# Softmax sums of a unit's pairs in one block of matmuls, V's product by row halves, output tiles copied by two engines

## The chip, the cores and the metric

The kernel runs on one core of a Trainium2 chip. The metric is the device time of one execution in microseconds (us), as the median of several runs.

## What is computed

Attention with normalised queries and keys over 8 batches of 12 heads, 448 positions and 64 columns a head, and behind it a two-layer block with the activation h cos h:

```python
q_n = q / (norm(q) + 1e-06); k_n = k / (norm(k) + 1e-06)     # 8 x 12 x 448 x 64
attn = softmax(q_n @ k_n^T / tau)                            # tau = 0.1
x = (attn @ v) as rows of 768                                # 3584 x 768
h = x @ w_in                                                 # 768 x 2048
out = (h * cos(h)) @ w_out                                   # 2048 x 768, float32
```

## The kernel before

**Tiling.** A pair (index g, 48 of them) is two heads of one batch; three pairs make a unit (index u, 16), two units a batch (8). A sequence of 448 positions is cut into 7 blocks of 64. Six of them lie as three full chunks of 128 partitions in the tile PX (two blocks in a chunk), the seventh is spread over the two partition halves, each half holding it for half of the queries (chunk 0 in the code, view PHv, 224 columns a head).

**A pair.** `scores(g, c)` multiplies keys and queries on TensorE as four 64\*64 tiles, c = 0 for the short chunk and 1 to 3 for the full ones, into two PSUM buffers SC in turn. ScalarE takes the exponential from SC to PX (line 707). `attend(g, direct, stages)` then forms V's product and the softmax sums in the two-bank PSUM buffer AV (AVa and AVs): stages 0 and 1 are the short chunk (`rest`, line 730: V and a block of ones, 64\*64), stage 2 is V's product over the full chunks in 128\*32 column tiles (`av`, line 737) and the sums of the full chunks with ones as weights (`sm` and `sm2`, lines 745 and 753, also 128\*32). One copy of both banks, 896 wide, goes to the tile xu: on VectorE (line 817), or for the even pairs above 18 on ScalarE (line 814).

**The chain.** For the pairs not in `PLAN["direct"]`, `chain(u)` collects a unit's sums: four gather DMAs on SyncE's queue from xu to sums (line 855), an addition of two parts and a reciprocal on VectorE (lines 867 and 870; in unit 2 on GpSimd), a write to DRAM (scr, line 871), two broadcast reads into RB (line 873), and for each pair GpSimd's multiply xT = xu x RB (line 877). The direct pairs take logarithm and exponential on ScalarE instead. Some of them, in `PLAN["quarters"]`, form V's product and the sums as 64\*64 tiles by row halves (`quarter`, line 763); the pairs in `PLAN["folded"]`, at the start, form half-wide sums (`sm32`, line 771).

**The two layers.** M1 (`m1`, matmuls in line 887) multiplies a batch's xT with w_in; ScalarE's Sin (line 916) and VectorE's product (line 918) give gT. Two of M1's column groups start early, with the first three chunks of xT; their other chunks follow as xT comes. M2 multiplies gT with w_out, 32 groups of matmuls to a tile of 128 rows, in 64\*64 tiles by row halves (`m2_quarters`, line 985) or as whole tiles (line 1014). `m2_drain` copies a finished tile in two halves of 384 columns to osb on VectorE (line 952; the last of all on ScalarE, line 950), and SyncE's queue stores it. osb has three buffers.

**Order.** `pair(g, f)` writes out the order on TensorE: scores of pair g, parts of `attend(g - 1)`, and between them the shares f[0] to f[3] of M2's groups (for a middle pair 3, 2, 5 and 6). All instructions are first collected with modelled costs; `play` then plays them through and fixes each engine's order by due times. On TensorE it keeps the written order, except in the first part of the kernel (`free`), where it looks 24 operations ahead.

Of the kernel before, what the change touches and what calls it, by code (L numbers as in the profile page):

```python
# [7 lines left out]
ALU = mybir.AluOpType  # L8
# [7 lines left out]
    "ahead": (1, 2),  # L16
    "folded": (0, 1, 2, 3),
# [45 lines left out]
class Program:  # L63
# [9 lines left out]
    WINDOW = 24  # L73
    PATIENCE = 0.1
# [81 lines left out]
    def play(self):  # L156
# [63 lines left out]
        while todo:  # L220
            best = None
            for e in self.ENGINES:
                if e == "PE":
                    s = None
                    for o in pe[: self.WINDOW if pe and pe[0].free else 1]:
                        if o.free != pe[0].free:
                            break
                        if left[o.idx] == 0:
                            t = max(free[e], ready_at[o.idx])
                            if s is None or t < s - self.PATIENCE:  # L230
                                s, c = t, (t, 0, o)
# [25 lines left out]
            if e == "PE":  # L257
                pe.remove(o)
                if o.free:
                    self.gaps.append((max(free[e], 3.0), s))  # L260
                if mode is not None and mode != o.mode:
# [129 lines left out]
def bass_cosine_attention__then__act_gcu_kernel(  # L391
# [22 lines left out]
    SPR = UH * S // 128  # L414
# [4 lines left out]
    NT = 3  # L419
    TD, LT = PLAN["turned"], 9  # L420
# [27 lines left out]
    lnn = sbs("lnn", 2, [128, UH * NB], F32)  # L448
# [7 lines left out]
    sums = sbs("sums", 2, [128, 2 * SPR], F32)  # L456
    rcp = sbs("rcp", 2, [128, SPR], F32)
# [14 lines left out]
    scr = nc.dram_tensor("scr", (NU, UH * S), F32)  # L472
# [10 lines left out]
    xuv = xu.ap().rearrange("p (r g s) -> p r g s", r=5, g=UP)  # L483
# [16 lines left out]
    ISSUE = {"load": (0.62, 128), "gather": (0.64, 64), "spread": (0.4, 128), "bcast": (0.62, 64),  # L500
# [48 lines left out]
    pool(lambda e: e.memset(ones.ap().rearrange("p (x y) -> p x y", y=32)[:, 0:4:3], 0.0), (), ["zeros"], 0.12)  # L549
    sel = [gT.bitcast(F32).ap()[:, (f * RING + S) // 2 : (f * RING + S) // 2 + 128] for f in (NF - 2, NF - 1)]  # L550
# [65 lines left out]
    lnnv = [t.ap().rearrange("p (h s) -> p h s", h=UH) for t in lnn]  # L616
    rnv = [t.ap().rearrange("p (h s) -> p h s", h=UH) for t in rn]

    def rnorm(u, p0, p1, t=(0, 1)):
# [5 lines left out]
        if u in PLAN["roots"]:  # L625
# [6 lines left out]
        act(lambda e: e.activation(lnnv[i][:, h, w], n2v[i][:, h, w], ACT.Ln, bias=cst.ap()[:, 1:2]),  # L632
            [("n2", i, p, z) for p, z in keys] + ["cst1"], [("lnn", i, p, z) for p, z in keys],
            n, "E", 1, "ln" + tag)
        act(lambda e: e.activation(rnv[i][:, h, w], lnnv[i][:, h, w], ACT.Exp, scale=-0.5),  # L635
            [("lnn", i, p, z) for p, z in keys], [("rn", i, p, z) for p, z in keys], n, "E", 0, "rn" + tag)
# [47 lines left out]
    def scores(g, c):  # L684
        j, y, z = g % 2, g % NT, (c + 1) % 2
# [25 lines left out]

    def attend(g, direct, stages=(0, 1, 2)):
        u, p, j = g // UP, g % UP, g % 2
        i, y, b = u % 2, u % 3, g // PB
        AVq = AVv[:, :, 0:S].rearrange("p x (s o m) -> p x s o m", s=NB, o=2)
        ws = slice(32, 96) if direct else slice(64, 128)
# [17 lines left out]
        def av(e, c):  # L734
# [4 lines left out]
            return t  # L739

        def sm(e):
            for n in range(2):
                for a in range(2):
                    o = 64 * a + 32 * n
                    t = e.matmul(AVv[o : o + 32, 1, 0:S], ones.ap()[:, 32:64], PXv[j][:, n, a, :],
                                 start=False, stop=False)
            return t

        def sm2(e):
            for n in range(2):  # L750
                for a in range(2):
                    o, w = 64 * a + 32 * n, slice(S // 2 * n, S // 2 * n + S // 2)
                    t = e.matmul(AVv[o : o + 32, 1, w], ones.ap()[:, 32:64], PXv[j][:, 2, a, w],  # L753
                                 start=False, stop=True)
            return t
# [52 lines left out]
        if not direct:  # L808
            P.op("PE", sm, ["ones", ("PX", j, 1), ("PX", j, 2)], ["AVs"], cost=MM, mode="C32", label="S%d" % g)
            P.op("PE", sm2, ["ones", ("PX", j, 3)], ["AVs"], cost=HALF, mode="C32", label="S%d" % g)  # L810
            keep = [("xa", u % 3, p), ("xs", i, p)]
            both = bass.AP(xu, (u % 3 * UP + p) * S, [[5 * UP * S, 128], [(3 + i - u % 3) * UP * S, 2], [1, S]])
            if g % 2 == 0 and g > 3 * PB:
                act(lambda e: e.activation(both, AVv[:, :, 0:S], ACT.Copy, bias=0.0), ["AVa", "AVs"], keep, 2 * S,
                    label="xu%d" % g)
            else:
                dve(lambda e: e.tensor_copy(both, AVv[:, :, 0:S]), ["AVa", "AVs"], keep, 2 * S, label="xu%d" % g)  # L817
            return
# [3 lines left out]
        if folded:  # L822
            s, r = xuv[:, 3 + i, p, 0 : S // 2], RBv[i][:, p, 0 : S // 2]
            act(lambda e: e.activation(s, AVv[:, 1, 0 : S // 2], ACT.Ln), ["AVs"], [("xs", i, p)], S // 2, "E",
                label="lnS%d" % g, bias=PLAN["bs"])
            act(lambda e: e.activation(r, s, ACT.Exp, scale=-1.0), [("xs", i, p)], [("RB", i, p)], S // 2, "E",
# [11 lines left out]
        act(lambda e: e.activation(xuv[:, 3 + i, p, :], AVv[:, 1, 0:S], ACT.Ln), ["AVs"], [("xs", i, p)], S, "E",  # L838
            label="lnS%d" % g, bias=PLAN["bs"] if g < PB else 0.0)
        act(lambda e: e.activation(r, xuv[:, 3 + i, p, :], ACT.Exp, scale=-1.0), [("xs", i, p)], [("RB", i, p)], S, "E",  # L840
# [10 lines left out]
    def chain(u):  # L851
        i, b = u % 2, u // 2
        n = sum(UP * u + p not in PLAN["direct"] for p in range(UP))
        w = SPR // UP * n
        dma("SP", [lambda e, r=r, a=a: e.dma_start(
            sums[i].ap()[64 * a : 64 * a + 64, w * r : w * r + w],
            bass.AP(xu, ((64 * a + 32 * r) * 5 + 3 + i) * UP * S, [[5 * UP * S, 1], [w, 64], [1, w]]))
            for r in range(2) for a in range(2)], [("xs", i, p) for p in range(n)], [("sums", i)], "sums%d" % i, 0.7,
            "gather%d" % u, pad=0.0 if u in PLAN["power"] else PLAN["late"])
        r = rcp[i].ap()[:, 0:w]  # L860
        parts = sums[i].ap()[:, 0 : 2 * w].rearrange("p (r x) -> p r x", r=2)
        if u in PLAN["power"]:
            pool(lambda e: e.tensor_tensor(r, parts[:, 0], parts[:, 1], ALU.add), [("sums", i)], [("rcp", i)], 0.23, label="sum")
            pool(lambda e: e.tensor_tensor(r, r, bass.AP(cst, 2, [[4, 128], [0, w]]), ALU.pow), [("rcp", i), "cst2"], [("rcp", i)],
                 0.05 + 0.166 * w, label="recip")
        else:
            dve(lambda e: e.tensor_reduce(out=r, in_=sums[i].ap()[:, 0 : 2 * w].rearrange("p (r x) -> p x r", r=2),
                                          axis=mybir.AxisListType.X, op=ALU.add), [("sums", i)], [("rcp", i)], 2 * w,
# [205 lines left out]
    def direct(g):  # L1074
        return g in PLAN["direct"]
# [179 lines left out]
```

## Time and profile before

| | |
|---|---|
| median of 3 runs | 425.53 us (424.62 to 425.71) |
| profiled execution | span 424.5 us, first to last instruction; no other time is given for it |
| TensorE (PE) | busy 414.0 us, 98% of the span, 6077 matmuls |
| ScalarE (ACT) | 274.1 us, 65% |
| GpSimd (POOL) | 236.9 us, 56% |
| VectorE (DVE) | 189.0 us, 45% |
| DMA | 63.61 MB, 150 GB/s on average |

The span is what lies between the first and the last instruction. Engines work side by side, so their busy times do not add up. A matmul's length holds the time in which it flows through the array while the next one has started; the cost of a series is read from the starts.

### The profile page before, as it was taken

What the parts mean: (1) busy time and instruction counts of PE and PEld (TensorE: products, weight loads), DVE (VectorE), ACT (ScalarE), POOL (GpSimd) and SP (SyncE); (2) the same over time, 40 slices, a digit from 0 to 9 for tenths busy, and PEclk for the clock granted to TensorE, in tenths of its full rate; (3) what the DMA queues carried; (4) which work ended last, traced back from release to release, by engine and by line L of the source; (5) the groups of instructions that cost most, each with busy time, mean ns of one, the idle gap of its engine ahead of it and who ended that gap; (6) DMA issues with size and microseconds to landing.
All of it is one profiled execution on the core that took longest, in us unless ns stands there. A gap on an engine that the chain in (4) does not pass through costs nothing.

```text
span 424.5 us, 13591 instructions
## 1 busy us (share of the span) xinstructions
PE 414.0 (98%) x6077; PEld 234.8 (55%) x6077; DVE 189.0 (45%) x250; ACT 274.1 (65%) x363; POOL 236.9 (56%) x189
## 2 busy tenths in 40 slices
PE   8899989999999999999999999999999999999997
PEld 3454556655556555655566455655566545555565
DVE  4564744555653086225733078122852144223521
ACT  5896578884897557876588556775488735713500
POOL 4999996897833794927493395806856042020000
PEclk9999999999999999999999999999999999999999
DMA  8999999999576999589655996569955930141023
GB/s 188 250 253 224 207 215 161 195 206 231 102 107 144 201 223 186 116 193 209 155 116 86 207 229 106 133 100 224 224 111 89 147 105 2 42 120 38 2 60 90
DMA packets 81034, 63.61 MB, mean 150 GB/s; under 512 B 45776, under 2 KB 75984, under 8 KB 80976
## 3 DMA queue, kind: packets, MB, share of 16 engines
q1 hardware_dynamic: 62768, 50.06, 56.8%
q0 software_dynamic: 18048, 12.59, 19.7%
q8 instruction: 48, 0.79, 0.8%
q10 hardware_dynamic: 160, 0.10, 0.1%
q14 instruction: 10, 0.08, 0.1%
HBM read 54.98 MB, written 11.13 MB: 156 GB/s over the span
## 4 chain that ended last, share of the span: by engine, by line
PE 73%; POOL 8%; DMA 6%; issue 4%; ACT 4%; SPq 3%; DVE 2%; ACTq 0%; POOLq 0%; DVEq 0%
PE MP L985 18%; PE SC L887 17%; PE AV L887 11%; PE SC L692 5%; PE AV L737 5%; POOL qks L643 4%; PE MP L1014 4%; POOL xT L877 3%; PE SC L1014 3%; DMA RB<-scr 3%; PE MP L887 2%; PE AV L730 2%; PE AV L763 1%; DMA qkT<-qks 1%; ACT PX L707 1%
## 5 line engine op out<-in xcount | busy, mean ns | idle before, releaser
L707 ACT ACTIVATE PX<-SC 128x448 bf16<-128x448 f32 (+1 forms) x192 | 153.2, 823 | 25.8 <-PE SC L692 15.6
L985 PE MATMUL MP<-W,gT 64*64 64x384 bf16 x2816 | 142.0, 323 | 0.8 <-DVE qkT L681 0.6
L985 PEld LDWEIGHTS MP<-W,gT 64*64 64x64 bf16 x2816 | 78.7, 107 | 34.5 <-issue 3.5
L643 POOL TENSOR_TENSOR qks<-raw,rn 128x896 bf16<-128x896 f32 (+1 forms) x48 | 79.6, 1680 | 31.8 <-ACT rn L635 31.6
L887 PE MATMUL SC<-xT,W 128*128 128x448 bf16 x444 | 90.2, 352 | 0.0
L877 POOL TENSOR_TENSOR xT<-xu,RB 128x448 bf16<-128x448 f32 x34 | 37.7, 1136 | 74.7 <-DMA RB<-scr 74.7
L604 POOL TENSOR_TENSOR sq<-raw 128x896 bf16<-128x896 f32 x44 | 73.8, 1694 | 8.3 <-DMA raw<-in_q_dram 7.7
L916 ACT ACTIVATE cosb<-SC,cst 128x896 f32<-128x896 f32 x37 | 37.2, 1006 | 49.0 <-PE SC L887 44.5
L887 PEld LDWEIGHTS SC<-xT,W 128*128 128x128 bf16 x444 | 43.4, 98 | 40.2
L887 PE MATMUL AV<-xT,W 128*128 128x448 bf16 x276 | 59.7, 353 | 1.7 <-POOL xT L877 1.7
L952 DVE COPY osb<-MP 128x384 f32<-128x384 f32 x50 | 25.9, 552 | 67.0 <-PE MP L985 56.4
L611 DVE TENSOR_REDUCE n<-sq 128x14 f32<-128x896 bf16 (+2 forms) x49 | 51.4, 1055 | 6.3 <-ACT sq L602 5.2
L692 PE MATMUL SC<-qkT 64*64 64x448 bf16 x576 | 52.1, 357 | 0.4 <-ACT PX L707 0.2
L918 DVE TENSOR_TENSOR gT<-SC,cosb 128x896 bf16<-128x896 f32 x37 | 40.3, 1088 | 23.2 <-ACT cosb L916 23.1
L916 ACT ACTIVATE cosb<-AV,cst 128x896 f32<-128x896 f32 x23 | 23.1, 1006 | 35.0 <-PE AV L887 32.0
L887 PEld LDWEIGHTS AV<-xT,W 128*128 128x128 bf16 x276 | 26.0, 98 | 29.1 <-POOL xT L877 5.1
L918 DVE TENSOR_TENSOR gT<-AV,cosb 128x896 bf16<-128x896 f32 x23 | 25.0, 1088 | 27.5 <-ACT cosb L916 27.4
L817 DVE COPY xu<-AV 128x896 f32<-128x896 f32 x20 | 21.7, 1083 | 30.4 <-PE AV L753 30.3
L737 PE MATMUL AV<-PX,va 128*32 128x448 bf16 x492 | 31.0, 356 | 0.0
L692 PEld LDWEIGHTS SC<-qkT 64*64 64x64 bf16 x576 | 16.5, 105 | 17.8 <-ACT PX L707 9.9
L730 PE MATMUL AV<-PX,va 64*64 64x224 bf16 x192 | 25.7, 262 | 0.2
L730 PE MATMUL AV<-PX,ones 64*64 64x224 bf16 x192 | 25.7, 262 | 0.0
(78 smaller groups left out, 361.7 us busy)
## 6 DMA issues: line engine op xcount, KB each, us to landing
raw<-in_k_dram SPq DMA_DIRECT2D x48, 224.0 KB, 6.4
raw<-in_q_dram SPq DMA_DIRECT2D x48, 224.0 KB, 7.1
out_dram<-osb SPq DMA_DIRECT2D x54, 192.0 KB, 3.4
va<-in_v_dram POOLq DMA_DIRECT2D x32, 192.0 KB, 8.9
RB<-scr SPq DMA_DIRECT2D x18, 336.0 KB, 4.8
W<-in_moe_w_in_dram POOLq DMA_DIRECT2D x4, 768.0 KB, 14.5
W<-in_moe_w_out_dram POOLq DMA_DIRECT2D x4, 768.0 KB, 19.1
RB<-scr SPq DMA_DIRECT2D x6, 224.0 KB, 4.3
```

Source lines behind the costliest of these rows:

```text
L604: pool(lambda e, x=x, y=y: e.tensor_tensor(y, x, x, ALU.mult), src_, dst, 0.1 + n * 1.78e-3, label="sq%d.%d" % (u, p)).pad = LATE if u > 1 ...
L611: dve(lambda e, w=w: e.tensor_reduce(out=n2v[i][:, 2 * p : 2 * p + 2, w], in_=sqv[p][:, :, w, :], axis=mybir.AxisListType.X, op=ALU.add), ...
L643: f = lambda e, s0=s0, s1=s1: e.tensor_tensor(qksv[i][:, p, s0:s1].rearrange("p s h d -> p h s d"), rawv[i][:, h, s0:s1, :], bass.AP(rn[i] ...
L692: m = e.matmul(SCv[z][BP * o : BP * o + BP, a, 0:S], t[r, c - 1 + (NT3 + 1) * o, 0:BP], t[r, :, BP : 2 * BP], start=True, stop=True)
L707: act(lambda e: e.activation(PHv[j] if c == 0 else PXv[j][:, c - 1], SCv[z][:, :, 0:n], ACT.Exp, scale=1.0 / TAU), ["SC%d" % z], [("PX", j ...
L730: m = e.matmul(to, w, PHv[j][r, a, :], start=(n == 0 and g not in PLAN["quarters"]), stop=False)
L737: t = e.matmul(AVv[o : o + 32, 0, 0:S], vav[y][:, 2 * p + a, c + 1, d : d + 32], PXv[j][:, c, a, :], start=False, stop=(c == NT3 - 1))
L877: pool(lambda e, p=p: e.tensor_tensor(xTv[b % 2][:, UP * i + p, :], xuv[:, u % 3, p, :], RBv[i][:, p, :], ALU.mult), [("RB", i, p), ("xa", ...
L887: t = e.matmul(ph[:, a, 0:S], W1v[:, order[c], 128 * n : 128 * n + 128], xTv[b % 2][:, order[c], :], start=(c == 0), stop=(c == NKC - 1))
L916: act(lambda e, ph=ph, cz=cz: e.activation(cosv[cz], ph[:, :, 0:S], ACT.Sin, bias=cst.ap()[:, 0:1], scale=1.0), names(gi) + ["cst0"], [("c ...
L918: dve(lambda e, ph=ph, cz=cz, gi=gi: e.tensor_tensor(gTv[:, 2 * gi : 2 * gi + 2, S * (b % 2) : S * (b % 2) + S], ph[:, :, 0:S], cosv[cz], ...
L985: r = e.matmul(POH[b][x : x + 64, 0:HW], gTv[k, y, col + x : col + x + 64], W2v[k, y, HW * b : HW * b + HW], start=(y == 0 and h == 0), st ...
```

## The change

For the pairs that are not direct:

- V's product over the full chunks is formed in 64\*64 tiles, each half of the partitions into its own bank of AV, and the short chunk joins each bank (`split`). VectorE copies the first bank to xu and then adds the second.
- The sums are no longer formed with each pair. When a unit's last such pair has its product, `counts(u)` forms the sums of all of them, one behind the other, in one 128 by 32 column tiling: each 32-column tile holds one head and one half of the queries, 224 columns; the weight (`mark`) has ones in a few columns, so that each pair's sums land in rows of their own. One copy of 224 columns goes to xs.
- The chain then needs one gather and no addition; RB holds the halves of the queries apart, and GpSimd's multiply reads and writes by pieces of 32.
- PX has four buffers instead of two (the exponentials stay until the unit's end). Room comes from xu (3 rows for 5), osb (2 buffers for 3), the logarithms in place, and zeros that share gT.
- For output tiles 0 to 24 ScalarE copies the second half.
- `play` may take any ready one of the next 8 TensorE operations outside the free part too, and charges a change of tiling in the choice. The written order moves: f[0] and f[1] are done together before the second score, and the third score comes before stage 2.

```diff
 PLAN = {
+    "halves": tuple(range(25)),
...
+    REACH = 8
...
-                    for o in pe[: self.WINDOW if pe and pe[0].free else 1]:
+                    for o in pe[: self.WINDOW if pe and pe[0].free else self.REACH]:
                         if o.free != pe[0].free:
                             break
                         if left[o.idx] == 0:
                             t = max(free[e], ready_at[o.idx])
+                            if not o.free and mode is not None and o.mode != mode:
+                                t += self.SWITCH[o.mode]
...
-    lnn = sbs("lnn", 2, [128, UH * NB], F32)
-    PX = sbs("PX", 2, [128, NB * S], BF16)
-    xu = sb("xu", [128, 5 * UP * S], F32)
+    PX = sbs("PX", NPX, [128, NB * S], BF16)
+    xu = sb("xu", [128, 3 * UP * S], F32)
+    xs = sbs("xs", 2, [128, S // 2], F32)
-    osb = sbs("osb", 3, [128, DM], F32)
+    osb = sbs("osb", NO, [128, DM], F32)
-    zt = sb("zt", [128, S], BF16)
+    zt = gT.ap()[:, S : 2 * S]
+    mark = sb("mark", [128, 3 * 4 * 32], BF16)
...
+    dve(lambda e: e.memset(mark.ap(), 0.0), (), ["mark0"], 192)
+    for z in range(2):
+        for n, at in enumerate(((0, 24), (0, 16, 24), (8,), (16,))):
+            for x in at:
+                dve(lambda e, ...: e.memset(markv[64 * z : 64 * z + 64, 0 : z + 2 : z + 1, n, x : x + 1], 1.0), ["mark0"], ["mark"], 8)
...
+    def split(g, stages):
...
+        def tail(e):
+            for o in range(2):
+                r = slice(BP * o, BP * o + BP)
+                for a in range(2):
+                    m = e.matmul(AVq[64 * a : 64 * a + 64, o, :, o, :], vav[y][r, 2 * p + a, 0 if o else VS - 1, :],
+                                 PHv[j][r, a, :], start=False, stop=True)
+        def part(e, c):
+            for o in range(2):
+                r = slice(BP * o, BP * o + BP)
+                for a in range(2):
+                    m = e.matmul(AVv[64 * a : 64 * a + 64, o, 0:S], vav[y][r, 2 * p + a, c + 1, :], PXv[j][r, c, a, :],
+                                 start=(c == 0), stop=False)
...
+            dve(lambda e: e.tensor_copy(to, AVv[:, 0, 0:S]), ["AVa"], [("xa", u % 3, p)], S, label="xa%d" % g)
+            dve(lambda e: e.tensor_tensor(to, to, AVv[:, 1, 0:S], ALU.add), ["AVs", ("xa", u % 3, p)], [("xa", u % 3, p)], S, label="xb%d" % g)
+    def counts(u):
+        gs = [UP * u + p for p in range(UP) if UP * u + p not in PLAN["direct"]]
+        for p, g in enumerate(gs):
+            def count(e, p=p, j=g % NPX):
+                v = p + 1 if p else len(gs) == 2
+                for c in range(-1, NT3):
+                    for o in range(4):
+                        a, h = o // 2, o % 2
+                        m = e.matmul(AVv[32 * o : 32 * o + 32, 0, 0 : S // 2], markv[:, 0 if c >= 0 else 1 + h, v, :],
+                                     halved(j, c, a, h) if c >= 0 else PHv[j][:, a, :],
+                                     start=(p == 0 and c < 0), stop=(p == len(gs) - 1 and c == NT3 - 1))
+        dve(lambda e: e.tensor_copy(xs[u % 2].ap(), AVv[:, 0, 0 : S // 2]), ["AVa"], [("xs", u % 2)], S // 2, label="xs%d" % u)
...
     def attend(g, direct, stages=(0, 1, 2)):
+        if not direct:
+            split(g, stages)
+            return
...
-        if not direct:
-            P.op("PE", sm, ["ones", ("PX", j, 1), ("PX", j, 2)], ["AVs"], cost=MM, mode="C32", label="S%d" % g)
-            P.op("PE", sm2, ["ones", ("PX", j, 3)], ["AVs"], cost=HALF, mode="C32", label="S%d" % g)
-            if g % 2 == 0 and g > 3 * PB:
-                act(lambda e: e.activation(both, AVv[:, :, 0:S], ACT.Copy, bias=0.0), ["AVa", "AVs"], keep, 2 * S,
-            else:
-                dve(lambda e: e.tensor_copy(both, AVv[:, :, 0:S]), ["AVa", "AVs"], keep, 2 * S, label="xu%d" % g)
...
     def chain(u):
-        dma("SP", [lambda e, r=r, a=a: e.dma_start(sums[...], bass.AP(xu, ...)) for r in range(2) for a in range(2)], ...)
+        dma("SP", [lambda e: e.dma_start(sums[i].ap()[:, 0:w], bass.AP(
+            xs[i], 0, [[128 // rows * (S // 2), rows], [w, S // 2 // w], [1, w]]))], [("xs", i)], [("sums", i)], "sums%d" % i, 0.7,
-            dve(lambda e: e.tensor_reduce(out=r, in_=sums[i] ..., op=ALU.add), ..., label="sum")
-            dve(lambda e: e.reciprocal(r, r), [("rcp", i)], [("rcp", i)], 8 * w, label="recip")
+            dve(lambda e: e.reciprocal(r, sums[i].ap()[:, 0:w]), [("sums", i)], [("rcp", i)], 8 * w, label="recip")
-            RBv[i][64 * a : 64 * a + 64, 0:n], bass.AP(scr, u * UH * S + a * n * S, [[0, 64], [1, n * S]])) for a in range(2)],
+            RB[i].ap()[64 * a : 64 * a + 64, 0 : n * S].rearrange("p (h x) -> p h x", h=2),
+            bass.AP(scr, u * 8 * S + a * rows * S // 4, [[0, 64], [rows * S // 8, 2], [1, n * S // 2]])) for a in range(2)],
...
     def m2_drain(t, hf, name, po, w):
-        o, n, ends = t % 3, w[1] - w[0], t == B * S // 128 - 1
+        o, n, ends = t % NO, w[1] - w[0], t == B * S // 128 - 1
-        if ends and w[1] == DM:
+        if w[1] == DM and (ends or t in PLAN["halves"]):
             act(lambda e: e.activation(dst, po[:, 0:n], ACT.Copy, bias=0.0), ...)
...
     def pair(g, f):
+        if late and not direct(g - 1):
+            f = (f[0] + f[1], 0) + f[2:]
...
+        elif late:
+            attend(g - 1, False, (1,))
             m2_fill(f[1], quarters)
-            attend(g - 1, direct(g - 1), (2,))
+            if not f[1]:
+                scores(g, 2)
+            attend(g - 1, False, (2,))
+        closes = g > PB and not direct(g - 1) and (g % UP == 0 or direct(g))
+        if closes:
+            m2_fill(f[2], quarters)
+            counts((g - 1) // UP)
...
-    zero = dve(lambda e: e.memset(zt.ap(), 0.0), (), ["zt"], S)
+    zero = dve(lambda e: e.memset(zt, 0.0), (), ["zt", ("gT", 1, 0)], S, bias=-1000.0)
```

More of the change, by code (lines that the diff above doesn't have):

```diff
@@ L260, in play @@
                     self.gaps.append((max(free[e], 3.0), s))
-                if mode is not None and mode != o.mode:
+                if o.free and mode is not None and mode != o.mode:
                     s += self.SWITCH[o.mode]
@@ new lines, in halved @@
+    def halved(j, c, a, o):
+        return PXv[j][:, c, a, :].rearrange("p (s o m) -> p s o m", s=NB, o=2)[:, :, o, :]
+    def counts(u):
[9 more added lines that the diff above has]
+                                     start=(p == 0 and c < 0), stop=(p == len(gs) - 1 and c == NT3 - 1))
+                return m
+            P.op("PE", count, ["mark"] + [("PX", g % NPX, c) for c in range(NT3 + 1)], ["AVa"], cost=(NT3 + 1) * HALF,
+                 mode="C32", label="S%d" % g)
+        dve(lambda e: e.tensor_copy(xs[u % 2].ap(), AVv[:, 0, 0 : S // 2]), ["AVa"], [("xs", u % 2)], S // 2, label="xs%d" % u)
@@ L853, in chain @@
         n = sum(UP * u + p not in PLAN["direct"] for p in range(UP))
[L854 to L858, printed above, removed]
+        rows = 16 if n > 1 else 4
+        w = rows * S // 256
@@ L1124, in pair @@
             attend(g - 1, direct(g - 1))
+        closes = g > PB and not direct(g - 1) and (g % UP == 0 or direct(g))
+        if closes:
+            if f[1]:
+                scores(g, 2)
+            m2_fill(f[2], quarters)
+            counts((g - 1) // UP)
         if g >= 1 and g != PB:
-            if g > PB and not direct(g - 1) and (g % UP == 0 or direct(g)):
+            if closes:
                 chain((g - 1) // UP)
@@ L1148, in pair @@
             load_v(3, None, [PLAN["v3"][1]])
-        if not late or g - 1 not in PLAN["quarters"]:
-            scores(g, 2)
-        m2_fill(f[2], quarters)
+        if not closes:
+            if not late or direct(g - 1) and g - 1 not in PLAN["quarters"] or not direct(g - 1) and f[1]:
+                scores(g, 2)
+            m2_fill(f[2], quarters)
         scores(g, 3)
@@ L1218, in bass_cosine_attention__then__act_gcu_kernel @@
     P.arrange()
-    P.emit(nc, ["out%d" % o for o in range(3)] + ["last"])
+    P.emit(nc, ["out%d" % o for o in range(NO)] + ["last"])
     ctx.close()
```

99 lines of the change are left out of this document (45 added, 54 removed).

## The prediction

> **What bounds the kernel now.** I read the page's busy shares and clock, then the waits of TensorE's matmuls and weight loads (PEld), then one pair of heads in TensorE's timeline.
>
> ```profile
> PE 414.0 (98%) x6077; PEld 234.8 (55%) x6077; DVE 189.0 (45%) x250; ACT 274.1 (65%) x363; POOL 236.9 (56%) x189
> ...
> PEclk9999999999999999999999999999999999999999
> ```
> ```profile
> PE MP L1044 <- DVE zt L1043: 1.9, 1, 1.9
> ...
> PEld MP L985 <- DVE osb L952: 2.5, 13, 0.2
> ...
> PE AV L887 <- POOL xT L877: 1.7, 7, 0.6
> ```
>
> TensorE is busy for 414.0 of 424.5 us at the full granted clock. Its first wait is the start of the program; of the matmuls' others the largest is on GpSimd's normalised xT, 1.7 us in seven waits. So the other engines do not set the end: the length of TensorE's instruction stream does. What a change takes out of that stream comes off the end, if nothing new makes it wait. "Busy" hides something, though: neighbouring matmuls overlap, so the cost of a group must be read from start to start. This is one pair in the middle of the kernel, whose softmax sums come from lines 745 and 753 (columns: start, length, engine, line, operation, tile sizes, count; the last row is ScalarE's copy of its result):
>
> ```profile
> 224.65 0.26 PE L730 MATMUL AV<-PX,va 64*64 64x224 bf16 x1
> ...
> 224.75 0.27 PE L700 MATMUL SC<-qkT 64*64 64x224 bf16 x4
> ...
> 225.61 0.49 PE L985 MATMUL MP<-W,gT 64*64 64x384 bf16 x8
> 226.04 0.75 PE L737 MATMUL AV<-PX,va 128*32 128x448 bf16 x12
> 226.62 0.36 PE L745 MATMUL AV<-PX,ones 128*32 128x448 bf16 x4
> 226.81 0.27 PE L753 MATMUL AV<-PX,ones 128*32 128x224 bf16 x4
> 227.01 0.38 PE L692 MATMUL SC<-qkT 64*64 64x448 bf16 x4
> 227.31 1.01 PE L985 MATMUL MP<-W,gT 64*64 64x384 bf16 x20
> ...
> 229.31 0.26 PE L730 MATMUL AV<-PX,va 64*64 64x224 bf16 x1
> ```
> ```profile
> 227.13 0.92 ACT L814 ACTIVATE xu<-AV 128x896 f32<-128x896 f32 x1 [0.47 <-PE AV L753]
> ```
>
> The next pair starts 4.66 us after this one. Four 64*64 matmuls of 224 columns take 0.10 us (224.65 to 224.75). The eight M2 matmuls from 225.61 are two groups. Their pace: from 227.31 to 229.31 run 20 and, behind one group of scores of 0.19, 24 more, so 1.81/11 = 0.165 us per group of four. These two groups end at 225.94, and the 128*32 matmuls of V's product start at 226.04: 0.10 us of nothing. V's product takes 0.58 (226.04 to 226.62), the sums 0.19 and then a short group, whose 0.10 would end at 226.91; the 64*64 score starts at 227.01, again 0.10 late. **Each visit to the 128*32 tiling costs 0.20 us, 0.10 on either side.** Between two 64*64 kinds there is no such gap.
>
> **The change, part by part.** How many pairs and units it touches:
>
> ```profile
> L753 PE MATMUL AV<-PX,ones 128*32 128x224 bf16 x136 | 9.2, 259 | 0.0
> ```
> ```profile
> L871 SPq DMA_DIRECT2D scr<-rcp x13: 326/340/597, 71.2 to 372.8; - x13
> ```
>
> Four short sums matmuls for each pair make 136/4 = 34 pairs that are normalised by the chain through DRAM; 13 writes to scr make 13 units. The pairs marked direct keep their code.
>
> *V's product as row halves* is the form that the quarter pairs have already, 64*64 with 448 columns, four to a group:
>
> ```profile
> 66.29 0.35 PE L763 MATMUL AV<-PX,va 64*64 64x448 bf16 x2
> ...
> 66.67 0.35 PE L763 MATMUL AV<-PX,va 64*64 64x448 bf16 x2
> ...
> 66.86 0.33 PE L985 MATMUL MP<-W,gT 64*64 64x384 bf16 x4
> ```
>
> Three groups take 0.57 (66.29 to 66.86), and 66.67 to 66.86 shows no gap to the M2 group behind them. Against 0.58 for the 128*32 form that is 0.01 less a pair. Two short 64*64 groups for the seventh chunk (V and ones mixed) become one: 0.10 less.
>
> *The sums* become four groups of four half-wide 128*32 matmuls a pair. The folded pairs of the start have that form:
>
> ```profile
> 18.14 0.46 PE L771 MATMUL AV<-PX,ones 128*32 128x224 bf16 x12
> 18.53 0.29 PE L700 MATMUL SC<-qkT 64*64 64x224 bf16 x4
> ```
>
> Twelve of them run from 18.14 to 18.53, with the 0.10 of leaving the tiling in it: 0.29/3 = 0.097 a group, 0.39 for four. That replaces the 0.19 + 0.10 = 0.29 of lines 745 and 753. Columns in all: 0.39 - 0.29 - 0.10 - 0.01 = -0.01 a pair, -0.3 us over 34. Four more instructions a pair are in these paces.
>
> *The visits to the 128*32 tiling* go from one for each of 34 pairs to one for each of 13 units: 21 x 0.20 = 4.2 us less. This is the core of the forecast. Its upper bound: the matmuls of V's product last 0.353 us each at a pace of 0.19, so a switch with no overlap at all would cost 0.16 a side and 6.7 us would go. Its lower bound is nothing, if the planner splits the blocks (a rival below).
>
> *VectorE* gets two passes of 448 for each pair in place of one of 896, and one of 224 for each unit; it gives up half of the output copies and the small reductions of the chains.
>
> ```profile
> L611 DVE TENSOR_REDUCE n<-sq 128x14 f32<-128x896 bf16 x47 | 50.2, 1074 | 2.3 <-ACT sq L602 1.2 <-POOL sq L604 1.0
> ...
> L952 DVE COPY osb<-MP 128x384 f32<-128x384 f32 x50 | 25.9, 552 | 67.0 <-PE MP L985 56.4 <-PE MP L1014 10.6
> ...
> L817 DVE COPY xu<-AV 128x896 f32<-128x896 f32 x20 | 21.7, 1083 | 30.4 <-PE AV L753 30.3
> ...
> L828 DVE COPY xu<-AV 128x448 f32<-128x448 f32 x4 | 2.5, 622 | 0.7 <-PE AV L737 0.6
> L830 DVE TENSOR_TENSOR xT<-xu,MP 128x448 bf16<-128x448 f32 x4 | 2.5, 621 | 4.1 <-PE MP L778 4.1
> ```
>
> A copy of 448 is 0.622 and an addition with one operand in PSUM 0.621 (lines 828 and 830 are just these), against 1.083 for the 20 wide copies. In sum 34 x 1.243 = 42.3, and 13 copies of 224 at about 0.39 (an estimate by the slope from 448 to 896) = 5.1; less 20 x 1.083 = 21.7 and 25 x 0.552 = 13.8. VectorE goes from 189.0 to about 201 us, less than half of the span: hidden. What matters is when the bank comes free. Now a copy starts 0.05 us behind the last matmul's end (226.81 + 0.27 to 227.13 above) and holds the bank for 0.92 or 1.08; then it will be 1.2. Until the next pair's first part of V's product stand five M2 groups, a score, and six M2 groups, as above: 11 x 0.165 + 0.19 = 2.0 us. The last matmul runs out for 0.2 beyond its slot, so 2.0 - 0.2 - 1.2 = 0.6 us stay. Covered, as long as VectorE is free at that moment; a 1.074 us reduction just started would cost up to 0.5 of TensorE's time. At a unit's end the sums block waits for the copy alone, 0.85 us against five groups' 0.82: even. The planner may now take any ready one of the next eight TensorE operations, which covers 0.1 and more.
>
> Here a rule of the Trainium skill speaks against the change. Its page "TensorEngine Tiling (Array Packing)", sections "PSUM Bottleneck" and "PSUM Pressure", says that tiling speeds up TensorE but not the emptying of PSUM, which can become the bottleneck, that row tiles need banks of their own, and that ScalarE and VectorE should share the emptying. Here V's product comes to need two banks and two passes of one engine. By it the time would be that of the second rival below; the DVE row of 45% and the 0.6 us above speak against it in this kernel.
>
> *ScalarE* loses 14 wide copies and gets 25 half output copies:
>
> ```profile
> L707 ACT ACTIVATE PX<-SC 128x896 bf16<-128x896 f32 x144 | 128.9, 916 | 20.6 <-PE SC L692 15.6
> ...
> L707 ACT ACTIVATE PX<-SC 128x448 bf16<-128x448 f32 x48 | 26.2, 545 | 5.2 <-PE SC L700 4.3
> ...
> L814 ACT ACTIVATE xu<-AV 128x896 f32<-128x896 f32 x14 | 12.8, 917 | 5.8 <-PE AV L753 5.6
> ```
> ```profile
> 105.00:144.00 39.00, 38.89 (x907) 23.50 (x910) 17.87 (x24) 33.27 (x46) 20.47 (x14) 1.00 0.75 132
> 209.00:238.00 29.00, 29.00 (x681) 17.94 (x684) 9.97 (x15) 23.96 (x33) 13.22 (x9) 1.00 0.58 123
> ```
>
> 14 x 0.917 = 12.8 less; 384 columns take 0.49 by the slope from 448 to 896: 25 x 0.49 = 12.2 more. Even in total. But the new copies fall also into the stage from 105 to 144 us, where ScalarE is already 85% busy and VectorE did all copies. Of 25 over the whole span some three fall in it, 1.5 us: 34.8 of about 37.5, still not the bound on average. The exponentials are also asked for closer together, since M2's second share moves ahead of the second score. The last score of a pair takes the bank of the second: behind that score's start lie 4 x 0.19 + 0.10 + 0.82 = 1.7 us of TensorE work, and its exponential is through after 0.19 + 0.05 + 0.92 = 1.2. An output copy of 0.49 in between just fits. I put 0.5 us of waits on it, between 0 and 25 x 0.1 = 2.5.
>
> *The chain of sums.* Before, in a unit whose last pair is copied at 222.58 (the chain of waits):
>
> ```profile
> 222.58 1.09 DVE L817 COPY xu<-AV 128x896 f32<-128x896 f32 x1 [4.53 <-PE AV L753]
> ```
> ```profile
> 225.38 0.59 SPq L855
> ...
> 226.01 1.99 DMA sums<-xu
> ...
> 228.02 0.21 DVE rcp L867
> ...
> 228.25 0.30 DVE rcp L870
> ```
>
> The wide copy ends at 223.67; the four gathers' issues last until 225.97, then come 1.99 to land, 0.21 of reduction, 0.30 of reciprocal. The change puts five M2 groups, 0.10, and three times 0.39 between V's product and the sums' copy: 0.82 + 0.10 + 1.17, then 0.05 + 0.39, where 1.1 stood: 1.4 us later. It saves three gather issues (about 1.7) and the reduction: 1.9 less. So the reciprocal is ready 0.5 us sooner. The first matmuls that need it stand three pairs later; these pairs carry two sums blocks (2 x 1.27) and lose three times 0.29 + 0.10 + 0.20 + 0.01: 0.7 us later. The waits of 1.7 us on xT should shrink by 0.5 to 1.2; I take 0.8, as landings vary by microseconds. The two broadcasts have twice the pieces at half the length; by their bytes nothing changes.
>
> ```profile
> L643 POOL TENSOR_TENSOR qks<-raw,rn 128x896 bf16<-128x896 f32 x47 | 78.6, 1693 | 31.5 <-ACT rn L635 31.3
> L604 POOL TENSOR_TENSOR sq<-raw 128x896 bf16<-128x896 f32 x44 | 73.8, 1694 | 8.3 <-DMA raw<-in_q_dram 7.7 <-DVE n L611 0.6
> L877 POOL TENSOR_TENSOR xT<-xu,RB 128x448 bf16<-128x448 f32 x34 | 37.7, 1136 | 74.7 <-DMA RB<-scr 74.7
> ```
>
> GpSimd's multiply gets pieces of 32 elements. Pieces of 64 (line 643) cost as much as whole rows (line 604), so I take 0. Were it a half more than the 1.136, the third multiply of a unit would end 1.7 us later, and three stages of M1 would wait that long: +5 at the far end; shorter pieces give nothing to gain.
>
> *The rest.* Two copying engines end an output tile sooner: in the pair above M2 restarts at 227.31 where the score ends at 227.20, behind two copies of 0.55 on VectorE; about 0.1, at the 13 places that the first row for PEld counts (2.5 us there, mostly hidden by matmuls still running). I take half, -0.6. Two output buffers instead of three: a tile lasts 32 x 0.165 = 5.3 us of M2 alone, which covers the store. The 15 new fills of constants lie where VectorE waits for the first data. Four buffers of exponentials only relax. Start and end stay.
>
> Sum: -0.3 - 4.2 - 0.8 - 0.6 + 0.5 (ScalarE) + 0.4 (VectorE: a reduction in the way costs 0.5 in one or two pairs, and the even case at the unit's end) = -5.0 us. Against the span of 424.5 that is 419.5; the runs' median 425.53 lies 1.0 above the span, so 420.5.
>
> **The rivals.** *More than that:* a switch costs near its upper bound, or the freer order fills the remaining waits too: -7.5, 418. For it the 0.353 against 0.19; against it that the starts show 0.10.
>
> *The bank of V's product becomes the bound.* Each pair's first part waits for VectorE's second pass. Place: between the addition and the next pair's first row half. It decides from the point where the mean wait exceeds (5.0 + 1.3)/34 = 0.19 us a pair. With a reduction in front of every drain it is 0.5 x 34 = 17, with one in front of half of them, and the sums block late by the same, 8.5 us: 425.5 - 5.0 + 8.5 = 429. For it: two passes, one engine, and a reduction lasts almost as long as both. Against it: from 209 to 238 us VectorE is busy for 9.97 of 29, and its reductions lie in the M1 stages; the copies stood waiting for TensorE.
>
> *ScalarE takes back half:* in the stages with 85% it comes out as the bound, 2.5 us there, and the chain is no sooner: 423.5. For it the row of 105 to 144, against it the lost 12.8 us.
>
> *The blocks don't stay blocks:* the planner, free to choose among eight operations, runs M2 or scores between the sums of a unit's pairs, so 34 visits stay: -5.0 + 4.2 = -0.8, 424.7. Against it: the three are ready together, and a change of mode is charged in the choice.
>
> **How the numbers follow.** This kernel's measurement can tell 0.3%, 1.3 us, from no change. Forecast 0.62 (own range 418.8 to 423), more 0.08, the bank 0.14, ScalarE 0.11, no blocks 0.05. Faster: 0.62 + 0.08 + about 0.06 of ScalarE = 0.76. Same: the rest of ScalarE and the blocks, 0.10. Slower: 0.14, with the multiply's far end in it. The range goes from 416.5 (6.7 instead of 4.2 for the switches and no new waits) to 426.0, which leaves the bank's rival and a little below outside.
>
> **What would show it.** Right: TensorE's row of waits as short as now; sums matmuls in 13 blocks of 16, 32 or 48; 64*64 V groups with no gap before and after; a middle pair from 4.6 to about 4.35 on average; VectorE near 201, ScalarE near 274. Wrong: new waits of TensorE on VectorE at V's product, or on ScalarE at the scores (the bank, ScalarE); over 13 visits (no blocks); xT waits over 2 us (the chain, the multiply); gaps around the row-half groups, which would undo the core of the sum.

## The result, and the profile after

The changed kernel takes 420.46 us (median of 4 runs, 419.66 to 421.65) against 425.07 (424.31 to 425.71): ratio 0.989, 95% interval 0.9863 to 0.9918. That is 4.6 us less, where 5.0 were forecast. The profiled executions differ by 4.7 us in span, 424.5 to 419.8.

The busy shares of the page after, then four rows of its waits (who waited, for whom: us in total, times, longest):

```profile
PE 410.2 (98%) x6213; PEld 251.1 (60%) x6213; DVE 201.4 (48%) x289; ACT 268.9 (64%) x374; POOL 236.7 (56%) x188
```
```profile
DVE xs L770 <- PE AV L764: 12.0, 13, 1.2
...
PEld MP L1020 <- ACT osb L984: 3.9, 14, 0.3
...
PE MP L1020 <- DVE gT L952: 1.4, 1, 1.4
```
```profile
PE AV L921 <- POOL xT L908: 0.2, 1, 0.2
```

TensorE is still the bound, 98% busy, 3.8 us shorter. The wait on xT has shrunk from 1.7 us to 0.2. The 13 copies of xs that wait for the sums matmuls are the 13 blocks. One row is new: M2 waits once for gT, 1.4 us. M2's weight loads now wait 14 times for ScalarE's output copy, where they waited 13 times, 2.5 us, for VectorE's before.

The unit that answers to the pair shown before, in TensorE's timeline (start, length, engine, line, tiles, count):

```profile
214.80 0.36 PE L740 MATMUL AV<-PX,va 64*64 64x448 bf16 x4
...
215.90 0.36 PE L703 MATMUL SC<-qkT 64*64 64x448 bf16 x4
...
216.47 0.36 PE L740 MATMUL AV<-PX,va 64*64 64x448 bf16 x4
216.66 0.27 PE L732 MATMUL AV<-PX,va 64*64 64x224 bf16 x4
216.90 1.01 PE L1020 MATMUL MP<-W,gT 64*64 64x384 bf16 x20
...
221.63 0.39 PE L703 MATMUL SC<-qkT 64*64 64x448 bf16 x4
221.95 1.33 PE L764 MATMUL AV<-PX,mark 128*32 128x224 bf16 x48
223.21 1.17 PE L1020 MATMUL MP<-W,gT 64*64 64x384 bf16 x24
224.21 0.36 PE L740 MATMUL AV<-PX,va 64*64 64x448 bf16 x4
...
228.28 0.39 PE L740 MATMUL AV<-PX,va 64*64 64x448 bf16 x4
```
```profile
216.19 0.56 DVE L987 COPY osb<-MP 128x384 f32<-128x384 f32 x1 [1.86 <-PE MP L1020]
```

One visit to the 128\*32 tiling remains: the score ends at 221.63 + 0.19 = 221.82 and the sums start at 221.95; 48 of them are 12 groups of 0.096, which end at 223.10, and M2 follows at 223.21. That is 0.13 and 0.11 around a block that serves three pairs. V's product (line 740) runs on at its pace, 216.47 to 216.66, with no gap. Behind its tail, though, M2 starts at 216.90 and not at 216.76: this is the start of a new output tile, whose banks VectorE and ScalarE empty from 216.19 on, 0.29 behind the end of the tile before (215.90). Three pairs last from 214.80 to 228.28, 13.48 us.

The new operations of VectorE, ScalarE's copy and GpSimd's multiply, by groups:

```profile
L750 DVE COPY xu<-AV 128x448 f32<-128x448 f32 x34 | 21.2, 624 | 43.3 <-PE AV L732 43.3
L751 DVE TENSOR_TENSOR xu<-xu,AV 128x448 f32<-128x448 f32 x34 | 21.0, 617 | 1.1
...
L770 DVE COPY xs<-AV 128x224 f32<-128x224 f32 x13 | 5.1, 392 | 12.0 <-PE AV L764 12.0
```
```profile
L984 ACT ACTIVATE osb<-MP 128x384 f32<-128x384 f32 x24 | 11.8, 491 | 14.2 <-PE MP L1049 7.1 <-PE MP L1020 7.0
```
```profile
L908 POOL TENSOR_TENSOR xT<-xu,RB 128x448 bf16<-128x448 f32 x34 | 37.7, 1135 | 61.5 <-DMA RB<-scr 61.5
```

All durations are as forecast: 0.624 and 0.617, 0.39 for xs, 0.49 for the output copy, and pieces of 32 cost GpSimd nothing (1135 ns, before 1136).

**Where the time came from.** I took the starts in TensorE's timeline from 57 to 368 us and subtracted from each distance the columns' pace (0.096, 0.189 and 0.1625 us for a group of four matmuls of 224, 448 and 384 columns, the same for a single one of the 128\*128 tiling). What is left is the gaps. Worked out so from the timelines, in us:

| gaps | before | after | one more visit | sums in 64\*64 | written order | one copier | before, look-ahead 8 |
|---|---|---|---|---|---|---|---|
| into and out of 128\*32 | 6.9 | 3.1 | 9.8 | 0.1 | 5.2 | 2.5 | 7.2 |
| within M1 (xT) | 3.0 | 0.3 | 2.4 | 3.9 | 0.0 | 0.3 | 0.7 |
| ahead of M2, from 64\*64 | 2.7 | 5.0 | 3.9 | 3.0 | 3.7 | 9.3 | 2.4 |
| all others | 5.3 | 5.0 | 3.6 | 7.1 | 6.0 | 6.7 | 4.2 |
| sum | 17.9 | 13.4 | 19.6 | 14.1 | 14.9 | 18.8 | 14.5 |
| span of this execution | 424.5 | 419.8 | 426.7 | 421.7 | 421.7 | 426.3 | 421.1 |

The gaps fall by 4.5 of the 4.7 us between the two executions. The first row gives 3.8 of it, xT 2.7, and M2 takes back 2.3. Each column is one execution, so a column explains the difference in span and not quite that of the medians. The border between the third and the fourth row depends on how the start of a group is taken, by up to 1 us.

The 2.3 us of M2 are two things. The larger is the one wait on gT:

```profile
209.34 0.38 PE L703 MATMUL SC<-qkT 64*64 64x448 bf16 x4
211.14 1.01 PE L1020 MATMUL MP<-W,gT 64*64 64x384 bf16 x20 [1.42 <-DVE gT L952]
```

M2 could have followed the score at 209.34 + 0.19 = 209.53 and starts at 211.14, 1.6 us later. The smaller is the start of the output tiles: ahead of the 21 tiles in this stretch lie 2.1 us of gaps before and 2.7 after.

### The profile page after: what moved, and what is told of

It is laid out like the page before. It is cut to its first block, busy times and chain, and to the rows that moved or that the text cites. A ratio compares the mean times of both kernels' runs of the same rounds, so it can differ in the third digit from the quotient of the medians.

```text
span 419.8 us, 13930 instructions
## 1 busy us (share of the span) xinstructions
PE 410.2 (98%) x6213; PEld 251.1 (60%) x6213; DVE 201.4 (48%) x289; ACT 268.9 (64%) x374; POOL 236.7 (56%) x188
## 4 chain that ended last, share of the span: by engine, by line
PE 81%; DMA 7%; SPq 4%; POOL 3%; DVE 2%; ACT 2%; issue 1%; ACTq 0%; DVEq 0%; POOLq 0%
PE MP L1020 25%; PE SC L921 17%; PE AV L921 10%; PE SC L703 6%; PE AV L740 4%; PE MP L1049 4%; PE AV L764 3%; PE SC L1049 3%; DMA sums<-xs 2%; PE AV L810 2%; PE MP L921 2%; SPq L671 2%; SPq L576 2%; POOL qks L654 2%; DMA RB<-scr 2%; DMA qkT<-qks 1%
## 5 line engine op out<-in xcount | busy, mean ns | idle before, releaser
L718 ACT ACTIVATE PX<-SC 128x448 bf16<-128x448 f32 (+1 forms) x192 | 149.6, 824 | 26.3 <-PE SC L711 13.5
L1020 PE MATMUL MP<-W,gT 64*64 64x384 bf16 x2816 | 138.1, 324 | 2.4 <-DVE gT L952 1.4
L1020 PEld LDWEIGHTS MP<-W,gT 64*64 64x64 bf16 x2816 | 84.4, 107 | 35.2 <-issue 5.7
L908 POOL TENSOR_TENSOR xT<-xu,RB 128x448 bf16<-128x448 f32 x34 | 37.7, 1135 | 61.5 <-DMA RB<-scr 61.5
L703 PE MATMUL SC<-qkT 64*64 64x448 bf16 x576 | 53.3, 353 | 0.2
L750 DVE COPY xu<-AV 128x448 f32<-128x448 f32 x34 | 21.2, 624 | 43.3 <-PE AV L732 43.3
L740 PE MATMUL AV<-PX,va 64*64 64x448 bf16 x408 | 36.9, 349 | 0.0
L987 DVE COPY osb<-MP 128x384 f32<-128x384 f32 x26 | 14.5, 558 | 46.4 <-PE MP L1020 35.2
L590 POOL DMA_DIRECT2D va<-in_v_dram x32 | 21.9, 689 | 6.3 <-DMA raw<-in_q_dram 4.1
L880 POOL TENSOR_TENSOR xT<-xu,RB 128x448 bf16<-128x448 f32 x8 | 9.1, 1136 | 27.4 <-ACT RB L876 27.4
L703 PEld LDWEIGHTS SC<-qkT 64*64 64x64 bf16 x576 | 18.0, 106 | 10.7 <-ACT PX L718 4.3
## 6 DMA issues: line engine op xcount, KB each, us to landing
W<-in_moe_w_in_dram POOLq DMA_DIRECT2D x4, 768.0 KB, 14.9
```

The source lines that it names most:

```text
L703: m = e.matmul(SCv[z][BP * o : BP * o + BP, a, 0:S], t[r, c - 1 + (NT3 + 1) * o, 0:BP], t[r, :, BP : 2 * BP], start=True, stop=True)
L718: act(lambda e: e.activation(PHv[j] if c == 0 else PXv[j][:, c - 1], SCv[z][:, :, 0:n], ACT.Exp, scale=1.0 / TAU), ["SC%d" % z], [("PX", j ...
L740: m = e.matmul(AVv[64 * a : 64 * a + 64, o, 0:S], vav[y][r, 2 * p + a, c + 1, :], PXv[j][r, c, a, :], start=(c == 0), stop=False)
L908: f = lambda e, p=p: e.tensor_tensor(xTv[b % 2][:, UP * i + p, :].rearrange("p (s o m) -> p o s m", s=NB, o=2), xuv[:, u % 3, p, :].rearra ...
L1020: r = e.matmul(POH[b][x : x + 64, 0:HW], gTv[k, y, col + x : col + x + 64], W2v[k, y, HW * b : HW * b + HW], start=(y == 0 and h == 0), st ...
```

## The experiments

Two theories stood against each other: the visits to the 128\*32 tiling are what was saved, or the freer order of TensorE is. The ratios are to the kernel before on the same chip; on the three chips used it took 425.6 to 426.4 us in the median. A ratio's interval is about 1 us to either side and that of the changed kernel as much, so that a difference of less than 1.5 us between two versions says nothing. What one part is worth is measured with the others in place, so these amounts don't add up to the 4.6 us. The moved written order was not tested by itself.

**The changed kernel again** (f1_after_again, no edit).

> The changed kernel once more, unchanged, so that it stands beside the others on one chip: 0.989 of the kernel before, 0.986 to 0.992.

0.9884 (0.9856 to 0.9911). The ratio for the others to be held against is 0.989.

**One more visit for each pair** (e1_visit).

```diff
+            for o in range(0, 128, 32):
+                a, d = o // 64, o % 64
+                m = e.matmul(AVv[o : o + 32, 0, 0:S], vav[y][:, 2 * p + a, 3, d : d + 32], PXv[j][:, 2, a, :],
-            P.op("PE", lambda e, c=n: part(e, c), ..., cost=MM, mode="Q", ...)
+            if n == 2: P.op("PE", whole, ..., cost=MM + 0.021, mode="C32", ...)
```

> The changed kernel, but the third full chunk of V's product goes into the first bank as one 128*32 group (as before the change) instead of a 64*64 group by row halves: each of 34 pairs visits the 128*32 tiling once more, columns stay the same. Theory of the visits (0.10 us on either side of each visit): 34 x (0.20 + 0.02) = 7.5 us more than the changed kernel, 428.0 us. Rival, the freer order of TensorE is what gains: the planner covers this, 420.5 to 421.5 us. Upper price of a switch (0.16 a side): 431.5 us.

1.0019 (0.9995 to 1.0042), 1.3% or 5.5 us over the changed kernel: the gain is gone with the same number of columns. The rival's 420.5 to 421.5 is out. The visit in its timeline:

```profile
220.13 0.36 PE L703 MATMUL SC<-qkT 64*64 64x448 bf16 x4
220.42 0.37 PE L747 MATMUL AV<-PX,va 128*32 128x448 bf16 x4
220.72 0.29 PE L732 MATMUL AV<-PX,va 64*64 64x224 bf16 x4
220.84 0.98 PE L1030 MATMUL MP<-W,gT 64*64 64x384 bf16 x20
```

The score ends at 220.32 and the 128\*32 group starts 0.10 later; it would end at 220.61, and the 64\*64 tail starts 0.11 later. The gaps on these sides grow by 6.7 us, 0.098 for each of 68 new sides; half a us less of other gaps, and the interval, lie between that and 5.5. The price of a visit is shown.

**The sums without a visit** (e2_counts64).

```diff
-                        m = e.matmul(AVv[32 * o : 32 * o + 32, 0, 0 : S // 2], markv[:, 0 if c >= 0 else 1 + h, v, :], ...
+                        m = e.matmul(AVv[64 * a : 64 * a + 64, o // 2, 0 : S // 2], ones.ap()[r, 32:96], ...
-                 mode="C32", label="S%d" % g)
+                 mode="Q", label="S%d" % g)
```

> The changed kernel, but the block of sums runs in the 64*64 tiling, so that no visit to 128*32 is left in the chained pairs. It leaves out the sums of the second half of the queries and the addition of the two row halves; matmuls and columns are as many as in the changed kernel. Theory of the visits: 13 x 0.21 = 2.7 us less, 417.8 us; up to 0.5 us of that may go to the wait for the second bank, which the block now writes too. Rival (order): 420.5 us.

0.9893 (0.9857 to 0.9929): no gain, where 2.7 us were expected. A miss for the time, not for the price: the sides' gaps went from 3.1 to 0.1 us as they should. But xT came too late:

```profile
PE AV L921 <- POOL xT L908: 1.7, 4, 1.2
...
PE MP L921 <- POOL xT L908: 1.2, 1, 1.2
```

2.9 us in five waits, where the changed kernel had 0.2. In the table the gaps within M1 grow by 3.6 us and all others by 2.1, while the wait on gT is missing here. So what was saved ahead of M1 turned in the main into waiting for the chain. That block also writes the second bank, and the plan moved; which of the two made xT late was not separated.

**The written order** (e3_reach1: REACH 1 for 8).

> The changed kernel with TensorE held to the written order again (REACH 1 for 8). Theory of the visits: the look-ahead covers small waits only, 421 to 422.5 us. Rival (order): the gain goes, 424 to 425.5 us.

0.9958 (0.9938 to 0.9979), 0.7% or 2.9 us over the changed kernel. That lies between the two theories' ranges: the look-ahead is worth more than "small waits only". Its profiled execution is 1.9 us longer in span; the gaps explain 1.5 us of that, and they grow where the prediction called it even, at the sums block behind VectorE's copy:

```profile
PE AV L764 <- DVE xu L750: 1.7, 3, 0.8
```

The gaps there grow from 3.1 to 5.2 us. TensorE does not wait for xT in this execution, so the shorter chain is enough for that without the look-ahead.

**The look-ahead alone, in the kernel before** (e7_before_reach8).

> The kernel before the change, with the planner's look-ahead of 8 on TensorE and the charge for a change of tiling in the choice, and nothing else. Theory of the visits: the 34 visits stay, 423.5 to 425.5 us (some waits of 1.7 us on xT may be covered). Rival (order): 421 to 422 us.

0.9971 (0.9955 to 0.9988), 1.2 us of 4.6, within the range of the first theory. The sides' gaps stay at 7.2 us; what falls is the wait on xT:

```profile
PE AV L890 <- POOL xT L880: 0.2, 1, 0.2
```

This execution was the fastest of twelve (422.88 us, the median 424.18): its gaps fall by 3.4 us, 2.3 of them on xT, more than the 1.2 us of the medians. So the freer order is worth 1.2 us by itself and some 2.9 on top of the rest, and it does not replace the visits.

**One engine for the output copies** (e4_onecopier: halves empty).

> The changed kernel with both halves of every output tile copied by VectorE. The prediction's term for two copying engines (0.6 us saved): 421.1 us. Rival, read from the trace of the changed kernel, where M2's weight loads wait 14 times for ScalarE's copy: the second engine saves nothing or costs, 419.5 to 420.5 us.

0.9992 (0.9972 to 1.0012): 1.0% or 4.3 us over the changed kernel. Both expectations miss, the rival's with the wrong sign. VectorE's copies of one tile, then TensorE behind them, and the row of TensorE's waits:

```profile
218.70 1.02 DVE L987 COPY osb<-MP 128x384 f32<-128x384 f32 x2 [1.86 <-PE MP L1020]
```
```profile
219.17 0.27 PE L732 MATMUL AV<-PX,va 64*64 64x224 bf16 x4
219.78 1.01 PE L1020 MATMUL MP<-W,gT 64*64 64x384 bf16 x20 [0.34 <-DVE osb L987]
```
```profile
PE MP L1020 <- DVE osb L987: 4.8, 13, 0.7
```

The tail would end at 219.27; M2 starts at 219.78, 0.06 behind the second copy. In the changed kernel the same place costs 0.14. The gaps ahead of M2 are 9.3 us for 5.0; those at the starts of the 21 output tiles are 8.1 for 2.7.

**Two engines in the kernel before** (f2_before_halves: the edit of `m2_drain` alone).

> The kernel before the change with the second half of output tiles 0 to 24 copied by ScalarE and nothing else. The prediction's term (0.6 us for two copiers): 0.998 to 0.999 of before. Theory now, from the run with one copier (1% over the changed kernel): two copiers are worth 4 us only in the changed order, where 0.86 us of other work lie between two tiles of M2 against 1.3 us before, so here again 0.5 us or less, 0.998 to 1.000; or worse, since ScalarE keeps its 14 wide copies and gets 12 us more, 1.002 to 1.006.

0.9985 (0.9966 to 1.0003): 0.6 us, the size of the prediction's term, but no change at all lies within the interval too. In its trace the gap ahead of eleven output tiles falls from 0.11 to 0.02 us; over the 21 tiles of the stretch it is 1.7 us for 2.1, 0.7 of it at a single tile. So the copies' second engine is worth 1.4 us at most in the old order and some 4 in the new one. The new order needs it: there only 0.86 us of work lie between two tiles.

**Longer use of the bank** (e5_pass1, e6_pass2: one or two further passes over AV ahead of the copy).

```diff
+            for n in range(1):   # 2 in e6_pass2
+                dve(lambda e: e.tensor_copy(to, AVv[:, 1, 0:S]), ["AVa", "AVs", ("xa", u % 3, p)], [("xa", u % 3, p)], S, label="xc%d" % g)
```

> The changed kernel with one more VectorE pass of 448 over V's product for each of the 34 pairs, ahead of the copy, so that both banks are held about 0.65 us longer. Theory of the visits, with the prediction's 0.6 us of slack behind each pair's drain: 420.5 to 422 us, and only the units' ends and the stage with reductions pay. Rival, the bank of V's product is the bound or close to it: 34 x 0.65 = 22 us more, 442 us.

> The changed kernel with two more such passes for each pair, both banks held about 1.3 us longer. If the slack is 0.6 us and the look-ahead covers 0.3 us more: 34 x 0.4 = 14 us more, 434 us; if the look-ahead covers the rest as well, 422 to 424 us. Bank as the bound: 34 x 1.3 = 44 us more, 465 us.

0.9972 (0.9945 to 0.9998) and 1.0106 (1.0078 to 1.0133): 3.5 and 9.2 us over the changed kernel. One pass of 0.65 for each of 34 pairs adds 21 us to VectorE and 3.5 to the time, some 2 us over the range for slack, far from the 442 of the bank as bound. The two profiled executions differ by 1.8 us in span and 1.4 in gaps, none of it within M1; the rest is not in these two. With two, the prediction's 0.6 us of slack are used up; yet of the 7.5 us of new gaps 4.3 lie within M1. It is again xT:

```profile
PE MP L923 <- POOL xT L910: 2.2, 2, 2.0
...
PE AV L923 <- POOL xT L910: 1.4, 4, 1.0
```

The bank is not the bound, and with the second pass the chain is what a longer drain hits most.

**Later places for the reciprocals** (e8_late6, f4_late1: PLAN late 6.0 and 1.0), an attempt to beat the changed kernel. The reason for it is M2's wait on gT: the copy of xs and SyncE's queue behind it, the chain of waits and VectorE's timeline up to that wait:

```profile
189.90 0.39 DVE L770 COPY xs<-AV 128x224 f32<-128x224 f32 x1 [1.23 <-PE AV L764]
```
```profile
193.37 0.72 SPq L576 DMA_DIRECT2D raw<-in_k_dram  x1
...
196.73 0.61 SPq L576 DMA_DIRECT2D raw<-in_q_dram  x1
197.44 2.19 SPq L991 DMA_DIRECT2D out_dram<-osb  x2
199.67 0.60 SPq L893 DMA_DIRECT2D sums<-xs  x1
```
```profile
199.67 8.13 DMA sums<-xs
```
```profile
207.82 0.33 DVE L900 RECIPROCAL rcp<-sums 128x28 f32<-128x28 f32 x1 [2.84 <-DMA sums<-xs]
208.07 1.03 DVE L952 TENSOR_TENSOR gT<-SC,cosb 128x896 bf16<-128x896 f32 x1
209.01 1.07 DVE L623 TENSOR_REDUCE n<-sq 128x14 f32<-128x896 bf16 x1
210.00 1.08 DVE L952 TENSOR_TENSOR gT<-AV,cosb 128x896 bf16<-128x896 f32 x1
```

The sums were ready at 190.29, but SyncE's queue stood on two transposes until 193.32 and then issued six loads and a tile's stores, so that the gather was issued at 199.67; by the chain it took 8.13 us. That the data of these loads held it up is likely, but not shown. The reciprocal stood next in VectorE's order and could not start before 207.82; the products of gT behind it came late (the last starts at 210.00), and M2 stood for 1.42 us.

> The changed kernel, planned with gathers that land 6 us later (PLAN late 6.0 for 0.0), so that VectorE's reciprocals come later in its order. In the trace of the changed kernel one gather took 8.1 us, the reciprocal at 207.8 us stood first in VectorE's queue, a product of gT waited behind it, and TensorE waited 1.42 us for that. Theory of this block: 1.0 to 1.5 us less, 419.0 to 419.5 us. Against it: the later reciprocals delay xT, whose waits return with 1 us or more, 421 to 422 us.

> The changed kernel with the gathers planned to land 1 us later (PLAN late 1.0 for 0.0; 6.0 had cost 24 us of waits on xT). If the reciprocal's place in VectorE's queue is what cost 1.4 us, and 1 us moves it: 0.986 to 0.988 of before. If the chain has no room left, waits on xT come back with it: 0.991 to 0.996.

1.0448 (1.0422 to 1.0475) and 0.993 (0.9907 to 0.9952). Both lose, and both in the main to xT:

```profile
PE AV L921 <- POOL xT L908: 13.7, 6, 4.4
```
```profile
PE AV L921 <- POOL xT L908: 2.6, 6, 1.6
```

With 6.0, all rows of waits on xT hold 15.4 us and the gaps within M1 21.9, for some 24 us more time; the second expectation took all of the 24 for waits on xT. M2's wait on gT moves from execution to execution: in the changed kernel run again it is 2.4 us in two places, the longer, 2.0, at 166.14, behind a reciprocal whose gather took 13.22 us by the chain. With 1.0 the reciprocal of the unit above comes at 214.18 and M2 no longer stands for it, but 1.3 us on gT stay at that other place; with 6.0 both are gone. The planner believes the number it is given and puts the reciprocals, and so xT, later for every unit, in order to spare such a wait at one or two.

**A longer look-ahead** (f3_reach16: REACH 16).

> The changed kernel with a look-ahead of 16 TensorE operations for 8. The look-ahead of 8 left no wait on ScalarE and 0.3 us on xT; if look-ahead covers waits and no more, 0.988 to 0.990 of before, as the changed kernel. If it pulls M2 forward to where it is missed later, 0.992 or more.

0.9896 (0.9868 to 0.9924), the same as the changed kernel. No version that was run beats it.

## Why the prediction was right

- **The core, 21 visits fewer at 0.20 us: right.** Forecast 4.2, gaps fell by 3.8; one more visit for each pair put 6.7 back. The upper price of 0.16 a side is out.
- **Columns even, V by row halves without gaps: right**, as the rows of line 740 show.
- **xT: right in sign, too small.** 0.8 forecast, 2.7 measured in M1's gaps (1.5 in the wait row). Two things do it, each nearly enough alone in the one execution that shows it: the shorter chain (written order: 0.0) and the look-ahead (kernel before with it: 0.7). I counted only the first.
- **Output tiles: the mis-sized term.** I took 0.6 us off for two copiers; the gaps at the starts of the tiles rose by 0.6, from 2.1 to 2.7. The reading of the old order was right (0.1 at a tile, and at eleven tiles two copiers take nearly all of it away there); the step that failed applied it to the new order, where less work lies between two tiles. Counting what stands between them in the new order (four groups of 0.19 and a tail of 0.10, 0.86 us, against 0.29 + 0.56 + 0.15 from the tile's end through VectorE's copy to M2's start) gives a wait of 0.14 even with two engines.
- **VectorE: 0.4 us allowed; what came was another thing.** The drain of V's product fits, and VectorE's busy time came out at 201.4. M2's 1.6 us on gT, behind a reciprocal, were not foreseen: I had moved the chain's start and saved a reduction without asking what is queued behind the reciprocal.
- **The total was luck in part.** xT gave 1.9 us more than forecast and ScalarE's 0.5 did not come; the tiles and gT took 1.2 each more, and the core gave 0.4 less. These errors nearly cancel, and the sum was better than its terms.
- **ScalarE: 0.5 us allowed, no wait of TensorE's matmuls on its exponentials over 0.4 us in all.** Its busy time fell from 274.1 to 268.9; the durations of its instructions, added up one by one, are 286.9 us in both, even as forecast. More of them overlap, and busy time counts an overlap once. The halved gain in its stages did not come.
- **The lower end of the range** was named for 6.7 us of switches and no new waits; by the prediction's own terms that is 417.1 and not 416.5.
- **A middle pair "to about 4.35" was wrong by the prediction's own sum.** 4.2 us over 34 pairs is 0.12 a pair; measured 13.48/3 = 4.49, with 4.66 for the pair shown before.
- **The rival of the bank fell**, as the two extra passes show, and with it what the Trainium skill's page "TensorEngine Tiling (Array Packing)", section "PSUM Bottleneck", would have made of the time. Its advice to use both ScalarE and VectorE for the emptying did hold, for another PSUM buffer: the output copies, 4.3 us in the new order.

## What to carry to other kernels

On a bound engine, read costs from start to start: the gap at a change of tiling shows in no busy time and in no row of waits, and it was the largest part of the gain. A term taken from the old order holds only where the order stays; recount what lies between a producer's end and its consumer in the new one. Once the stream is shorter, the next saving may go straight into a chain of transfers that used to be on time, so look at its slack before cutting further.

## What was not expected of the hardware

A gather issued behind six loads took 8.13 us by the chain of waits, another 13.22 in the unchanged kernel run again. The landings that the view of sums could match took 1.8 in the median and 3.8 at most. Such late gathers are not new: in the kernel before the same view has landings of up to 10.1 us, and VectorE stood longer for them (22.6 us for 5.6). New is M2's wait: VectorE's fixed order holds the products behind the reciprocal in both kernels, and the last one starts at 210.15 before and at 210.00 after, but M1 ends at 208.9 before and at 207.2 after, so that M2 comes to it sooner. The kernel before spread from 423.66 to 427.5 us over three sets of more than twenty executions, more than the 0.3% that I had taken from three.
